# Cross terms of a split-precision product: float32r operands exchanged for bfloat16 copies

## The chip, the core and the metric

The kernel runs on one core of a Trainium2 chip. The metric is device time in microseconds (us) of one execution. Its engines are called PE (TensorE, with PEld for its weight loads), ACT (ScalarE), DVE (VectorE), POOL (GpSimd) and SP (which issues the DMAs). Each of the four compute engines runs its own instruction list strictly in the order in which the kernel wrote it (`tc.add_manual_dep` at the end of the kernel pins that order); what lets engines wait for one another are semaphores.

## The reference

Two steps follow each other on 32,768 tokens of width 192: a short causal convolution whose seven taps are softmaxed per token and head, and a feed-forward layer whose activation is h·cos(h).

```python
# x: (8, 4096, 192), weight_gen: (8, 4096, 8 heads, 7 taps)
w = softmax(weight_gen, axis=-1)
out[b, s, head] = sum_k w[b, s, head, k] * x_pad[b, s + k, head]   # 6 rows of zeros ahead of x
h = out.reshape(32768, 192) @ w_in        # w_in: 192 x 2048
g = h * cos(h)
result = g @ w_out                        # w_out: 2048 x 192
```

`w_in` and `w_out` arrive as 64-bit floats; the kernel rebuilds each value as the sum of two 32-bit parts.

## The kernel before, in words

**Work and blocks.** The 32,768 rows are cut into 64 blocks (`NB`) of 512 rows (`CT`, four rows on each of 128 partitions). The hidden width 2048 is cut into 16 chunks of 128, taken two at a time: 8 pairs (`NPAIR`) for each block. One turn of the main loop (`for i in range(N + LAG + 1)`, `N` = 512) handles one pair of one block, and each engine gets a fixed list of instructions for it. I call such a turn an iteration.

**The two products.** Each operand is split into a high part (float32r, the precision that PE keeps of a 32-bit number) and a low part, the remainder. The first product h = x·w_in is then the sum high·high (the main term) and two cross terms, low x by high w and high x by low w. Since the contraction is 192 = 128 + 64 long and PE is used as two halves of 64 rows, `ffn_in_first` issues 3 pairs of matmuls and `ffn_in_second` 6 pairs, all 512 columns wide with 64 rows each; the two of a pair run in the two halves of PE at once. Of these 9 pairs an iteration, 3 are main terms (`wa_hi` or `wb_hi` by `x_hi`), and 6 are cross terms. `wa` holds the first contraction half-blocks of w_in, `wb` the middle one. The second product (`ffn_out`, L416, for the pair that was begun 6 iterations earlier) has 16 matmuls of 384 columns in float32r (`wo` by `ghi`) and 16 of 192 columns in bfloat16 (`wo_b` by `glo`).

**What happens to h.** h lies in PSUM (three buffers of two banks, `ps_h`). ACT rounds h + 0.25 to an integer (`act_turns`, L364), DVE subtracts (`dve_fraction`, L368), ACT takes the sine (`act_cos`, L372), DVE multiplies into h (`dve_g`, L375). An iteration later ACT writes the high part of g (`act_hi`, L382) and DVE the low part (`dve_lo`, L386), which frees the h buffer for PE.

**What happens to x.** POOL computes the convolution of later blocks (`attention`, L257 products and L272 sums, 13 instructions a block) and the softmax of 16 rows at a time (once in 4 blocks, with an Exp on ACT that costs two loads of its function table). PE transposes the result, one row of a block in each two iterations, into the last columns of the accumulator `acc` (L316). Every second iteration ACT copies `acc` to SBUF (`evacuate`, L439); in half of these cases POOL then adds it to the earlier half and stores it (L456, L457). In the iteration after the copy `split` makes the parts of the transposed row: ACT writes `x_hi` (L297, after its sine), POOL writes `x_lo` (L299, 128 x 256). Only the blocks 0, 1 and 2 are transposed and split as a whole (128 x 1024, with `x_lo` on DVE).

**Order on DVE and ACT.** In an iteration DVE runs L368, L386, L375; ACT runs L364, L382, L372, and behind these in turn L439 in one iteration and L297 in the next. Two iterations make the unit that repeats. I call the iteration with L439 A and the one with L297 and the split B.

**Weights.** `two_parts` turns the 64-bit words of a piece of w_in or w_out into parts: ACT, DVE three times, ACT for the high part (L143), for w_out a bfloat16 copy as well (L145), POOL for the low part (L146). w_in comes in seven such pieces, two before the first product, one more before the loop, the others in its first iterations.

Of the kernel before, what the change touches and what calls it, by code (L numbers as in the profile page):

```python
# [11 lines left out]
F32 = mybir.dt.float32  # L12
F32R = mybir.dt.float32r
I32 = mybir.dt.int32
U16 = mybir.dt.uint16
BF16 = mybir.dt.bfloat16
# [4 lines left out]
P = 128  # L21
# [22 lines left out]
def tile_softmax_conv_then_cos_ffn(  # L44
# [8 lines left out]
    nc = tc.nc  # L53
# [5 lines left out]
    F = w_in.shape[1]  # L59
# [4 lines left out]
    CT = R * P  # L64
# [12 lines left out]
    const = ctx.enter_context(tc.tile_pool(name="const", bufs=1))  # L77
    gpool = ctx.enter_context(tc.tile_pool(name="gpool", bufs=9))
    work = ctx.enter_context(tc.tile_pool(name="work", bufs=2))
# [13 lines left out]


    wa_hi = const.tile([P, F], F32R, name="wa_hi")
    wa_lo = const.tile([P, F], F32R, name="wa_lo")

    wb_hi = const.tile([P, F // 2], F32R, name="wb_hi")
    wb_lo = const.tile([P, F // 2], F32R, name="wb_lo")
    wo = const.tile([P, NFC, 2 * D], F32R, name="wo")  # L100
    wo_b = const.tile([P, NFC, D], BF16, name="wo_b")

    def words(n, home="ghi"):

        if home == "ghi":
            raw = gpool.tile([P, 2 * CW], I32, name="raw", tag=home)
        elif home == "fin":
            raw = work.tile([P, R * D], I32, name="raw", tag=home)
        else:
            raw = work.tile([P, 2 * CT], I32, name="raw", tag=home)  # L110
        return raw[:, 0:2 * n]
# [8 lines left out]
    def two_parts(raw, hi, lo, half=None):  # L120
        shape = hi.shape[1:]
        n = math.prod(shape)

        def shaped(t, steps):
            t = t.rearrange("p (n s) -> p n s", s=steps)
            return t if len(shape) == 1 else t.rearrange("p (a b) s -> p a b s", b=shape[1])

        low, top = (shaped(raw, 2)[..., k] for k in range(2))
        size, bits = (shaped(t[:, 0:n], 1)[..., 0] for t in room.pop(0))
        nc.scalar.activation(out=size.bitcast(F32), in_=top.bitcast(F32), func=AF.Abs, scale=F64_SCALE)  # L130
        yield
        nc.vector.tensor_scalar(
            out=size, in0=size, scalar1=3, scalar2=None, op0=ALU.logical_shift_left)
        yield

        nc.vector.scalar_tensor_tensor(
            out=size, in0=top, scalar=-0x80000000, in1=size, op0=ALU.bitwise_and, op1=ALU.bitwise_or)
        yield

        nc.vector.scalar_tensor_tensor(  # L140
            out=bits, in0=low, scalar=29, in1=size, op0=ALU.logical_shift_right, op1=ALU.bitwise_or)
        yield
        nc.scalar.copy(out=hi, in_=bits.bitcast(F32))  # L143
        if half is not None:
            nc.scalar.copy(out=half, in_=bits.bitcast(F32))  # L145
        nc.gpsimd.tensor_tensor(out=lo, in0=bits.bitcast(F32), in1=hi.bitcast(F32), op=ALU.subtract)  # L146

    def w_in_a(c0, c1, home="ghi"):
        raw = words(c1 - c0, home)
        for n in range(2):  # L150
            nc.sync.dma_start(out=raw[n * D2:(n + 1) * D2],
                              in_=w_in[n * P:n * P + D2, c0:c1].bitcast(I32))
        return two_parts(raw, wa_hi[:, c0:c1], wa_lo[:, c0:c1])

    w_in_odd_even = w_in.rearrange("k (a n c) -> n k a c", n=2, c=P)

    def w_in_b(j):
        raw = words(CW)
        pairs = slice(j * CW // P, (j + 1) * CW // P)
        for n in range(2):  # L160
            nc.sync.dma_start(out=raw[n * D2:(n + 1) * D2].rearrange("k (a c) -> k a c", c=2 * P),
                              in_=w_in_odd_even[1 - n, D2:P, pairs, :].bitcast(I32))
        cols = slice(j * CW, (j + 1) * CW)
        return two_parts(raw, wb_hi[:, cols], wb_lo[:, cols])

    w_out_v = w_out.rearrange("(c p) d -> p c d", p=P)

# [111 lines left out]
    xT, transposed = {}, set()  # L279

    def traded(t):

        nc.sync.keepalive_nop([nc.sync.lower_ap(t)])
# [4 lines left out]
    def parts_of(b):  # L288
        if b not in xT:
            hi = work.tile([P, 2, CT], F32R, name="x_hi")  # L290
            lo = work.tile([P, 2, CT], F32R, name="x_lo")
            xT[b] = (hi, lo)
        return xT[b]

    def split(b, t, cs, eng):
        hi, lo = parts_of(b)
        nc.scalar.copy(out=hi[:, :, cs], in_=t)  # L297
        yield
        eng.tensor_tensor(  # L299
            out=lo[:, :, cs], in0=t, in1=hi[:, :, cs].bitcast(F32), op=ALU.subtract)  # L300

# [23 lines left out]
    def chunk(pair, n):  # L325
        return slice((2 * pair + n) * P, (2 * pair + n + 1) * P)

    def ffn_in_first(i, h=None):

        b, pair = divmod(i, NPAIR)  # L330
        x_hi, x_lo = xT[b]
        if h is None:
            h = ps_h.tile([P, 2, CT], F32, name="h")
        for m, (w, v) in enumerate(((wa_hi, x_lo), (wa_lo, x_hi), (wa_hi, x_hi))):
            for q in range(2):
                rs = slice(q * D2, (q + 1) * D2)
                nc.tensor.matmul(  # L337
                    h[:, q, :], lhsT=w[rs, chunk(pair, q)], rhs=v[rs, q, :],
                    start=(m == 0), stop=False, skip_group_check=True)
        hs[i] = h  # L340
        traded(h)

    def ffn_in_second(i):

        b, pair = divmod(i, NPAIR)
        x_hi, x_lo = xT[b]
        h = hs[i]
        prods = ((wa_hi, x_lo, 0), (wa_lo, x_hi, 0), (wb_hi, x_lo, 1), (wb_lo, x_hi, 1),
                 (wa_hi, x_hi, 0), (wb_hi, x_hi, 1))
        for m, (w, v, middle) in enumerate(prods):  # L350
            for q in range(2):
                rs = slice(q * D2, (q + 1) * D2)
                cs = slice(pair * P, (pair + 1) * P) if middle else chunk(pair, 1 - q)
                nc.tensor.matmul(  # L354
                    h[:, 1 - q, :], lhsT=w[rs, cs], rhs=v[rs, q ^ middle, :],
                    start=False, stop=(m == len(prods) - 1), skip_group_check=True)
# [71 lines left out]
    def evacuate(j):  # L428
# [9 lines left out]
        if WHOLE < bt < NB:  # L438
            nc.scalar.copy(out=part, in_=acc)  # L439
            r = group % R  # L440
            splits.append(split(bt, part[:, :, 2 * D:], slice(r * P, (r + 1) * P), nc.gpsimd))
        else:
            nc.scalar.copy(out=part[:, :, 0:2 * D], in_=acc[:, :, 0:2 * D])
# [48 lines left out]
    def all_of(*steps):  # L492
# [4 lines left out]

    late = [
        (-1, 1, w_in_a, (768, 1280)), (-1, 2, w_in_b, (1,)), (-1, 2, w_out_2, (0,)),
        (0, 3, w_in_a, (1280, 1792)), (0, 3, w_out_2, (1,)), (1, 4, w_out_2, (2, "part1")),  # L500
        (1, 4, w_out_2, (3, "part1")), (2, 5, w_in_a, (1792, 2048, "fin")),
        (2, 5, w_out_2, (4, "fin")), (4, 6, w_out_2, (5, "part1")), (4, 7, w_out_2, (6, "part1")),
        (5, 8, w_out_2, (7, "fin")),
# [16 lines left out]
    next(sm0)  # L520
    load_rows(0)
    w_b0 = w_in_b(0)
    w_a0 = w_in_a(0, 256)
    sm1 = softmax(R, 3 * R, nc.gpsimd)
# [31 lines left out]
    go_on(w_a1, 1)  # L556
    all_of(mix_v)
    first = split(0, transpose_all(0), slice(0, CT), nc.vector)
    go_on(sm2, 2)
    go_on(w_a1, 3)  # L560
# [11 lines left out]
    for i in range(N + LAG + 1):  # L572
        b, pair = divmod(i, NPAIR)
# [20 lines left out]
        def products():  # L594
            if b < NB and pair == 0:
                assert b in transposed
            if whole is not None and j >= 0:

                ffn_out(j)
                ffn_in_first(i, whole)  # L600
            elif busy and EXP + 2 <= step <= EXP + 4:

                ffn_out(j, rest=False)
                ffn_in_first(i)
                ffn_out(j, rest=True)
            else:
                if i < N:
                    ffn_in_first(i, whole)
                if j >= 0:
                    ffn_out(j)  # L610
            if i < N:
                ffn_in_second(i)
            if j in stores:
                stores.pop(j)()
            if j >= 0:
                evacuate(j)
# [16 lines left out]
        if whole is not None:  # L633
            t = work.tile([P, 2, CT], F32, name="part0", bufs=3)
            nc.scalar.copy(out=t, in_=whole)
            later.append(split(b + 1, t, slice(0, CT), nc.vector))
# [64 lines left out]
```

## Time and profile before

| | |
|---|---|
| time, median of 3 runs | 2301.77 us (2301.21 to 2303.03) |
| span of the profiled execution, first to last instruction | 2300.3 us |
| the median less that span | 1.5 us |
| from the start to the first product | 28.45 us |
| 32 iterations (4 blocks) in the steady state | 138.41 us |
| repeated pieces of 32 iterations | about 15 |
| DVE instructions in a piece of 32 iterations | 99 |

Times in a timeline are a start and a duration in us, then the engine, the line of the kernel, the operation and `output<-inputs` with their shapes; a wait stands in brackets with the instruction that ended it. In the group rows the figures behind the bar are the busy time of the group in us and the mean duration of one instruction in ns, and behind the next bar the idle time ahead of them. PE's matmuls overlap one another, so the distance between their starts tells their cost, not the duration of one.

### The profile page before, as it was taken

The numbers are of one execution on the slowest core, as the hardware profiler recorded it, in microseconds if no ns is written. First come the engines' busy times: TensorE is split into PE (matmuls) and PEld (weight loads), VectorE is DVE, ScalarE is ACT, GpSimd is POOL, SyncE is SP. The second block draws the span as 40 slices with busy tenths as digits, with TensorE's granted clock in tenths as the row PEclk, the third lists the DMA queues.
The fourth block names the chain that finished last, engine by engine and source line by source line (L and its number), as shares of the span: only waits on it lengthen the run. The fifth ranks groups of instructions, "written<-read, shape, count | busy, mean of one in ns | idle before, by whom it ended". The sixth has DMA issues, their size and how long they took to land.

```text
span 2300.3 us, 60609 instructions
## 1 busy us (share of the span) xinstructions
PE 2215.2 (96%) x26504; PEld 1993.6 (87%) x26504; DVE 1905.0 (83%) x1646; ACT 1897.5 (82%) x2131; POOL 2002.3 (87%) x1461
## 2 busy tenths in 40 slices
PE   3799999999999999999999999999999999999998
PEld 2588998889888888998989988898888889899897
DVE  7788888888888888888888888888888888888886
ACT  4588888888888888888888888888888888888885
POOL 8699989999999989989899899989989899899840
PEclk8799999999999999999999999999999999999999
DMA  6211221211211211211211212212211212212100
GB/s 154 56 43 40 50 51 33 58 41 34 58 39 44 50 40 44 50 49 34 58 33 43 58 31 52 50 32 52 50 41 42 58 26 50 57 26 52 33 9 22
DMA packets 25767, 105.55 MB, mean 46 GB/s; under 512 B 2734, under 2 KB 6566, under 8 KB 25502
## 3 DMA queue, kind: packets, MB, share of 16 engines
q1 hardware_dynamic: 25502, 101.67, 18.5%
q8 instruction: 208, 3.41, 0.6%
q14 instruction: 57, 0.47, 0.1%
HBM read 76.50 MB, written 25.17 MB: 44 GB/s over the span
## 4 chain that ended last, share of the span: by engine, by line
PE 56%; POOL 22%; ACT 11%; DVE 7%; issue 4%; DMA 0%; SPq 0%; POOLq 0%; ACTq 0%; DVEq 0%
PE acc L416 26%; PE h L354 19%; PE h L337 10%; POOL pr L257 6%; POOL xa L272 6%; DVE turn L368 3%; ACT part L439 3%; ACT turn L364 3%; POOL part L456 3%; DVE glo L386 2%; POOL x_lo L299 2%; POOL xa L257 2%; POOL fin L457 2%; ACT turn L372 2%; ACT ghi L382 1%
## 5 line engine op out<-in xcount | busy, mean ns | idle before, releaser
L368 DVE TENSOR_TENSOR turn<-h,turn 128x1024 f32<-128x1024 f32 x512 | 625.8, 1222 | 309.9 <-ACT turn L364 309.9
L416 PE MATMUL acc<-wo,ghi 64*128 64x384 f32 x8144 | 815.2, 336 | 16.6 <-ACT part L439 13.5
L416 PEld LDWEIGHTS acc<-wo,ghi 64*128 64x128 f32 x8144 | 739.2, 185 | 64.2 <-ACT part L439 26.7
L272 POOL TENSOR_TENSOR xa<-xa,pr 128x768 f32<-128x768 f32 (+1 forms) x384 | 704.0, 1833 | 0.7
L372 ACT ACTIVATE turn<-turn 128x1024 f32<-128x1024 f32 x512 | 543.7, 1062 | 181.0 <-DVE turn L368 177.7
L375 DVE SCALAR_TENSOR_TENSOR h<-h,turn 128x1024 f32<-128x1024 f32 x512 | 631.0, 1232 | 54.2 <-ACT turn L372 54.2
L364 ACT ACTIVATE turn<-h 128x1024 int32<-128x1024 f32 x512 | 525.6, 1027 | 165.0 <-PE h L354 164.2
L386 DVE TENSOR_TENSOR glo<-h,ghi 128x1024 bf16<-128x1024 f32 x512 | 622.4, 1216 | 9.9 <-ACT ghi L382 9.9
L257 POOL TENSOR_TENSOR pr<-xt,taps 128x768 f32<-128x768 f32 (+1 forms) x384 | 588.2, 1532 | 11.9
L382 ACT CAST ghi<-h 128x1024 fp32r<-128x1024 f32 x512 | 518.2, 1012 | 15.5 <-DVE h L375 15.5
L416 PE MATMUL acc<-wo_b,glo 64*128 64x192 bf16 x8144 | 435.6, 243 | 0.0
L456 POOL TENSOR_TENSOR part<-part,part 128x768 f32<-128x768 f32 x126 | 233.0, 1849 | 183.0 <-ACT part L439 156.7
L416 PEld LDWEIGHTS <-glo 64*128 64x128 bf16 x8144 | 333.8, 94 | 28.5 <-issue 13.7
L337 PE MATMUL h<-x_lo,wa_hi 64*128 64x512 f32 x1024 | 216.4, 410 | 37.0 <-DVE glo L386 28.4
L354 PE MATMUL h<-x_lo,wa_hi 64*128 64x512 f32 x1024 | 251.1, 478 | 0.6
L439 ACT COPY part<-acc 128x1024 f32<-128x1024 f32 x244 | 242.9, 996 | 0.0
L354 PE MATMUL h<-x_lo,wb_hi 64*128 64x512 f32 x1024 | 209.4, 397 | 0.0
L354 PE MATMUL h<-x_hi,wa_hi 64*128 64x512 f32 x1024 | 209.1, 396 | 0.0
L337 PE MATMUL h<-x_hi,wa_hi 64*128 64x512 f32 x1024 | 208.1, 394 | 0.0
L337 PE MATMUL h<-x_hi,wa_lo 64*128 64x512 f32 x1024 | 207.4, 392 | 0.0
L354 PE MATMUL h<-x_hi,wb_hi 64*128 64x512 f32 x1024 | 206.9, 391 | 0.0
L354 PE MATMUL h<-x_hi,wb_lo 64*128 64x512 f32 x1024 | 206.4, 391 | 0.0
(69 smaller groups left out, 2097.7 us busy)
## 6 DMA issues: line engine op xcount, KB each, us to landing
xt<-in_x_dram SPq DMA_DIRECT2D x62, 960.0 KB, 6.9
out_dram<-fin SPq DMA_DIRECT2D x63, 384.0 KB, 3.4
taps<-in_weight_gen_dram SPq DMA_DIRECT2D x15, 448.0 KB, 4.7
raw<-in_moe_w_out_dram SPq DMA_DIRECT2D x8, 384.0 KB, 4.2
raw<-in_moe_w_in_dram SPq DMA_DIRECT2D x10, 256.0 KB, 10.0
xt<-in_x_dram SPq DMA_DIRECT2D x1, 768.0 KB, 10.3
xt<-in_x_dram SPq DMA_DIRECT2D x1, 540.0 KB, 5.7
raw<-in_moe_w_in_dram SPq DMA_DIRECT2D x4, 128.0 KB, 5.6
```

Source lines behind the costliest of these rows:

```text
L257: eng.tensor_tensor(out=dst.rearrange("p r (h g) -> p r h g", h=H), in0=xt[:, k + ra:k + rb, :].rearrange("p r (h g) -> p r h g", h=H), in ...
L272: eng.tensor_tensor(out=acc if k < K else xa, in0=acc, in1=old[:, ra:rb], op=ALU.add)
L337: nc.tensor.matmul(h[:, q, :], lhsT=w[rs, chunk(pair, q)], rhs=v[rs, q, :], start=(m == 0), stop=False, skip_group_check=True)
L354: nc.tensor.matmul(h[:, 1 - q, :], lhsT=w[rs, cs], rhs=v[rs, q ^ middle, :], start=False, stop=(m == len(prods) - 1), skip_group_check=True)
L364: nc.scalar.activation(out=t.bitcast(I32), in_=hs[i], func=AF.Identity, bias=0.25, scale=1.0)
L368: nc.vector.tensor_tensor(out=t, in0=hs[i], in1=t.bitcast(I32), op=ALU.subtract)
L372: nc.scalar.activation(out=t, in_=t, func=AF.Sin, bias=SIN_BIAS, scale=SIN_SCALE)
L375: nc.vector.scalar_tensor_tensor(out=hs[i], in0=hs[i], scalar=TWO_PI, in1=turns.pop(i), op0=ALU.mult, op1=ALU.mult)
L382: nc.scalar.copy(out=hi, in_=hs[i])
L386: nc.vector.tensor_tensor(out=lo, in0=hs.pop(i), in1=hi.bitcast(F32), op=ALU.subtract)
L416: nc.tensor.matmul(to, lhsT=g[rs, n, t * P:(t + 1) * P], rhs=w[rs, fc, :], start=(lo == 0 and c == 0 and (whole or s == 0)), stop=(lo == 1 ...
L439: nc.scalar.copy(out=part, in_=acc)
```

## The change

Low parts of x and of w_in are stored as bfloat16 instead of float32r. Beside them come bfloat16 copies of the high parts: `wa_b` and `wb_b` of the weights, written by ACT in `two_parts` (its argument `half` exists already for w_out), and `x_b` of x, written by DVE from `x_hi` in `split`. The cross terms take their operands from these: `wa_b` by `x_lo` and `wa_lo` by `x_b`, and so for `wb`. The main term stays as it is. The number and the shapes of the matmuls stay as they are.

```diff
-    wa_lo = const.tile([P, F], F32R, name="wa_lo")
+    wa_lo = const.tile([P, F], BF16, name="wa_lo")
+    wa_b = const.tile([P, F], BF16, name="wa_b")
...
-    wb_lo = const.tile([P, F // 2], F32R, name="wb_lo")
+    wb_lo = const.tile([P, F // 2], BF16, name="wb_lo")
+    wb_b = const.tile([P, F // 2], BF16, name="wb_b")
...
-        return two_parts(raw, wa_hi[:, c0:c1], wa_lo[:, c0:c1])
+        return two_parts(raw, wa_hi[:, c0:c1], wa_lo[:, c0:c1], wa_b[:, c0:c1])
...
     def parts_of(b):
...
-            lo = work.tile([P, 2, CT], F32R, name="x_lo")
-            xT[b] = (hi, lo)
+            lo = work.tile([P, 2, CT], BF16, name="x_lo")
+            near = work.tile([P, 2, CT], BF16, name="x_b")
+            xT[b] = (hi, lo, near)
...
     def split(b, t, cs, eng):
-        hi, lo = parts_of(b)
+        hi, lo, near = parts_of(b)
         nc.scalar.copy(out=hi[:, :, cs], in_=t)
         yield
+        nc.vector.tensor_copy(out=near[:, :, cs], in_=hi[:, :, cs].bitcast(F32))
         eng.tensor_tensor(
             out=lo[:, :, cs], in0=t, in1=hi[:, :, cs].bitcast(F32), op=ALU.subtract)
...
-        for m, (w, v) in enumerate(((wa_hi, x_lo), (wa_lo, x_hi), (wa_hi, x_hi))):
+        for m, (w, v) in enumerate(((wa_b, x_lo), (wa_lo, x_b), (wa_hi, x_hi))):
...
-        prods = ((wa_hi, x_lo, 0), (wa_lo, x_hi, 0), (wb_hi, x_lo, 1), (wb_lo, x_hi, 1),
+        prods = ((wa_b, x_lo, 0), (wa_lo, x_b, 0), (wb_b, x_lo, 1), (wb_lo, x_b, 1),
                  (wa_hi, x_hi, 0), (wb_hi, x_hi, 1))
```

Two places in the order of the instructions matter below. On DVE, in the steady state, this is an iteration A and an iteration B before; `turn`, `h`, `glo` and `ghi` are the tiles of the steps on h told above, with the number of the buffer.

```order
L386 TENSOR_TENSOR glo_16833<-h_16703,ghi_16832 128x1024
L375 SCALAR_TENSOR_TENSOR h_16768<-h_16768,turn_16830 128x1024
L368 TENSOR_TENSOR turn_16900<-h_16841,turn_16900 128x1024
L386 TENSOR_TENSOR glo_16903<-h_16768,ghi_16902 128x1024
L375 SCALAR_TENSOR_TENSOR h_16841<-h_16841,turn_16900 128x1024
L368 TENSOR_TENSOR turn_16970<-h_16909,turn_16970 128x1024
```

And now, in the lines of the changed file (L372, L390 and L379 there are L368, L386 and L375 of the kernel before):

```order
L390 TENSOR_TENSOR glo_16987<-h_16857,ghi_16986 128x1024
L379 SCALAR_TENSOR_TENSOR h_16922<-h_16922,turn_16984 128x1024
L302 CAST x_b_16571<-x_hi_16569 128x2x128
L372 TENSOR_TENSOR turn_17055<-h_16996,turn_17055 128x1024
L390 TENSOR_TENSOR glo_17058<-h_16922,ghi_17057 128x1024
L379 SCALAR_TENSOR_TENSOR h_16996<-h_16996,turn_17055 128x1024
L372 TENSOR_TENSOR turn_17125<-h_17064,turn_17125 128x1024
```

The cast to `x_b` is put between the last step of one iteration and the first of the next, once in two iterations; nothing else on DVE moves.

On PE this is the passage from the second product to `ffn_in_second` before.

```order
L416 MATMUL acc<-wo_b,glo 128x192
L354 MATMUL h<-x_lo,wa_hi 128x512 x2
L354 MATMUL h<-x_hi,wa_lo 128x512 x2
L354 MATMUL h<-x_lo,wb_hi 128x512 x2
L354 MATMUL h<-x_hi,wb_lo 128x512 x2
```

And now:

```order
L420 LDWEIGHTS glo
L420 MATMUL acc<-wo_b,glo 128x192
L358 LDWEIGHTS wa_b
L358 MATMUL h<-x_lo,wa_b 128x512
L358 LDWEIGHTS wa_b
L358 MATMUL h<-x_lo,wa_b 128x512
L358 LDWEIGHTS wa_lo
L358 MATMUL h<-x_b,wa_lo 128x512
```

The matmuls keep their order; those of the cross terms follow the bfloat16 matmuls of the second product directly, and their weight loads are now instructions of their own in the list (the trace shows a load for every matmul in both forms).

More of the change, by code (lines that the diff above doesn't have):

```diff
@@ L163, in w_in_b @@
         cols = slice(j * CW, (j + 1) * CW)
-        return two_parts(raw, wb_hi[:, cols], wb_lo[:, cols])
+        return two_parts(raw, wb_hi[:, cols], wb_lo[:, cols], wb_b[:, cols])
     w_out_v = w_out.rearrange("(c p) d -> p c d", p=P)
@@ L330, in ffn_in_first @@
         b, pair = divmod(i, NPAIR)
-        x_hi, x_lo = xT[b]
+        x_hi, x_lo, x_b = xT[b]
         if h is None:
             h = ps_h.tile([P, 2, CT], F32, name="h")
-        for m, (w, v) in enumerate(((wa_hi, x_lo), (wa_lo, x_hi), (wa_hi, x_hi))):
+        for m, (w, v) in enumerate(((wa_b, x_lo), (wa_lo, x_b), (wa_hi, x_hi))):
             for q in range(2):
@@ L345, in ffn_in_second @@
         b, pair = divmod(i, NPAIR)
-        x_hi, x_lo = xT[b]
+        x_hi, x_lo, x_b = xT[b]
         h = hs[i]
-        prods = ((wa_hi, x_lo, 0), (wa_lo, x_hi, 0), (wb_hi, x_lo, 1), (wb_lo, x_hi, 1),
+        prods = ((wa_b, x_lo, 0), (wa_lo, x_b, 0), (wb_b, x_lo, 1), (wb_lo, x_b, 1),
                  (wa_hi, x_hi, 0), (wb_hi, x_hi, 1))
```

## The prediction

> **What bounds the kernel now.** The page's busy times come first, then one steady piece of 32 iterations in the view of windows (columns: length, then busy time and count of PE, PEld, DVE, ACT, POOL, and PE's granted clock).
>
> ```profile
> PE 2215.2 (96%) x26504; PEld 1993.6 (87%) x26504; DVE 1905.0 (83%) x1646; ACT 1897.5 (82%) x2131; POOL 2002.3 (87%) x1461
> ...
> 1174.58:1312.99 138.41, 137.04 (x1664) 126.31 (x1665) 116.11 (x99) 117.54 (x132) 126.00 (x92) 1.00 0.19 45
> ```
>
> PE fills 137.04 of 138.41 us at full clock. All others are close behind, POOL at 126.00. So PE decides today, but not by much, and what counts is the rhythm in which the engines hand h on. PE's timeline of one iteration gives PE's own cost.
>
> ```profile
> 1200.04 1.57 PE L416 MATMUL acc<-wo,ghi 64*128 64x384 f32 x16
> ...
> 1201.51 0.82 PE L416 MATMUL acc<-wo_b,glo 64*128 64x192 bf16 x16
> 1202.11 0.48 PE L354 MATMUL h<-x_lo,wa_hi 64*128 64x512 f32 x2
> 1202.43 0.39 PE L354 MATMUL h<-x_hi,wa_lo 64*128 64x512 f32 x2
> ...
> 1204.29 1.57 PE L416 MATMUL acc<-wo,ghi 64*128 64x384 f32 x16
> ...
> 1206.36 0.48 PE L354 MATMUL h<-x_lo,wa_hi 64*128 64x512 f32 x2
> ```
>
> From 1202.11 to 1206.36 is one iteration: 4.25 us, so 32 of them take 136.0 and only 2.4 of the 138.41 are lost (around the Exp). The pairs of the first product start 1204.29 − 1202.43 = 1.86 us apart over 8 pairs, 0.2325 us each; the first one after bfloat16 work takes 1202.43 − 1202.11 = 0.32.
>
> The other rhythm is that of ACT and DVE. The timeline of an iteration A and the B after it, ACT and DVE alone:
>
> ```profile
> 1264.82 1.23 DVE L368 TENSOR_TENSOR turn<-h,turn 128x1024 f32<-128x1024 f32 x1 [0.66 <-ACT turn L364]
> ...
> 1266.08 1.06 ACT L372 ACTIVATE turn<-turn 128x1024 f32<-128x1024 f32 x1 [0.39 <-DVE turn L368]
> 1267.04 0.99 ACT L439 COPY part<-acc 128x1024 f32<-128x1024 f32 x1
> ...
> 1268.01 1.03 ACT L364 ACTIVATE turn<-h 128x1024 int32<-128x1024 f32 x1
> ...
> 1269.07 1.23 DVE L368 TENSOR_TENSOR turn<-h,turn 128x1024 f32<-128x1024 f32 x1 [0.66 <-ACT turn L364]
> ...
> 1270.21 1.21 DVE L386 TENSOR_TENSOR glo<-h,ghi 128x1024 bf16<-128x1024 f32 x1
> 1270.33 1.06 ACT L372 ACTIVATE turn<-turn 128x1024 f32<-128x1024 f32 x1 [0.38 <-DVE turn L368]
> ...
> 1271.42 1.23 DVE L375 SCALAR_TENSOR_TENSOR h<-h,turn 128x1024 f32<-128x1024 f32 x1
> ...
> 1273.31 1.23 DVE L368 TENSOR_TENSOR turn<-h,turn 128x1024 f32<-128x1024 f32 x1 [0.66 <-ACT turn L364]
> ```
>
> Follow who waits for whom: DVE L368, ACT L372, ACT L439, ACT L364, DVE L368, ACT L372, DVE L375. Each starts when the one ahead is done; there is no idle time in this chain. The next DVE instruction could start 1.15 us after L375 (as L386 does, 1.14 after L368), at 1272.57. So this chain needs 1272.57 − 1264.82 = 7.75 us for two iterations, while PE needs 8.50. The difference, 0.74 us ahead of the L368 at 1273.31, is spent waiting for PE through ACT. It is the only room in the chain, and the change puts its cast exactly there.
>
> **What PE gains.** A bfloat16 pair of 192 columns costs (0.82 − 0.243)/7 = 0.082 us, with 243 ns as the duration of one:
>
> ```profile
> L416 PE MATMUL acc<-wo_b,glo 64*128 64x192 bf16 x8144 | 435.6, 243 | 0.0
> ```
>
> No row has a bfloat16 pair of 512 columns. Scaled by columns it costs 0.082 × 512/192 = 0.219; the other bound is that it gains nothing, 0.2325. I take 0.22, near the bfloat16 row: 6 pairs × 0.0125 = 0.075 us an iteration. The 0.32 of the first pair goes too, since it now follows bfloat16 work with bfloat16 work: 0.0875 saved, of which 0.056 come back (today that pair starts 1202.11 − 1202.08 = 0.03 after the last bfloat16 pair, not 0.082). The sum is 0.105 us an iteration, between 0.03 and 0.11. PE would need 4.145, two iterations 8.29. The Trainium skill ("TensorE: Matmul & The Clock Gate", "Back-to-back issue gap") gives columns/2.4 + 2.5 ns, an estimate of 0.216 for 512 columns; by it PE would gain 0.13 an iteration. Its 0.0825 for 192 columns is what the row shows.
>
> **What DVE pays.** The cast, 128 x 256 from SBUF to SBUF, is not in this trace. Its nearest rows are DVE's other one-input instructions inside SBUF, L213 in the start, of 32, 64 and 128 elements: 182, 195 and 756 ns. Here is that line's answer, and DVE and POOL around the long one, and around another DVE instruction on SBUF alone:
>
> ```profile
> L213 DVE TENSOR_SCALAR den<-den x3: 182/195/756, 5.0 to 82.3; 128x32 f32<-128x32 f32 x1, 128x64 f32<-128x64 f32 x1, 128x128 f32<-128x128 f32 x1
> ...
> 82.27 0.76 DVE L213 TENSOR_SCALAR den<-den 128x128 f32<-128x128 f32 x1
> ...
> 78.33 4.61 POOL L272 TENSOR_TENSOR xa<-xa,pr 128x768 f32<-128x768 f32 x2
> ...
> 130.45 2.08 DVE L299 TENSOR_TENSOR x_lo<-part,x_hi 128x1024 fp32r<-128x1024 f32 x1
> ...
> 129.89 1.55 POOL L257 TENSOR_TENSOR xa<-xt,taps 128x768 f32<-128x768 f32 x1
> 131.41 4.02 POOL L257 TENSOR_TENSOR pr<-xt,taps 128x768 f32<-128x768 f32 x2
> ```
>
> The slope from 32 to 64 elements is 13 ns, so 128 should take some 220 ns, not 756. But POOL was inside an L272 that ended at 78.33 + 4.61 = 82.94, and DVE ended 0.09 after that. At 130.45 it is the same: POOL's instruction ends at 131.44, DVE's 1.09 later, and POOL's next pair takes 4.02 where two take 3.1. These DVE instructions and POOL's don't run side by side; the one that comes second waits for the other to end. The steps L368, L386 and L375, which have h in PSUM, show no such waits (1.21 to 1.23 throughout). So the question is what the cast meets, and it meets POOL nearly always:
>
> ```profile
> L272 POOL TENSOR_TENSOR xa<-xa,pr 128x768 f32<-128x768 f32 x378 | 700.5, 1853 | 0.6
> ...
> L257 POOL TENSOR_TENSOR pr<-xt,taps 128x768 f32<-128x768 f32 x378 | 585.1, 1548 | 11.9
> ...
> L456 POOL TENSOR_TENSOR part<-part,part 128x768 f32<-128x768 f32 x126 | 233.0, 1849 | 183.0 <-ACT part L439 156.7 <-ACT part L443 26.2
> ...
> L299 POOL TENSOR_TENSOR x_lo<-part,x_hi 128x256 fp32r<-128x256 f32 x244 | 179.7, 739 | 30.5 <-ACT x_hi L297 30.5
> L457 POOL TENSOR_TENSOR fin<-part 128x384 f32<-128x384 f32 x126 | 127.4, 1011 | 9.9
> ...
> L257 POOL TENSOR_TENSOR xa<-xt,taps 128x768 f32<-128x768 f32 x63 | 97.2, 1543 | 1.3
> ...
> L132 DVE TENSOR_SCALAR h<-h 128x256 int32<-128x256 int32 x2 | 0.9, 427 | 0.0
> ```
>
> A piece of 32 iterations is four blocks and holds 24 of L272, 28 of L257, 8 each of L456 and L457 and 16 of L299. For a cast that comes at any time, what is left of POOL's instruction is on average the sum of count × duration²/2 over the piece: (41.2 + 33.5 + 13.7 + 4.1 + 4.4)/138.4 = 0.70 us. The pair of iterations shown above would be one of the bad ones, since there the cast would come at 1272.57:
>
> ```profile
> 1272.52 1.55 POOL L257 TENSOR_TENSOR pr<-xt,taps 128x768 f32<-128x768 f32 x1
> ```
>
> After the wait, 256 elements at the slope of L213 (13 ns for 32) take 0.10; the long L213 took 0.09 after its wait where the slope gives 0.05, so I add 0.04 and say 0.15. One cast then costs the chain 0.70 + 0.15 − 0.08 (back-to-back DVE instructions overlap by that) = 0.77 us. Bounds: 0.19 if POOL is never met (0.27 − 0.08, from 182 ns plus 7 × 13), 0.35 if it also runs as slowly as L132 on 256 elements (427 ns less 0.08), and 1.9 if it met an L272 at its start each time. The Trainium skill ("SBUF — State Buffer", "Who interferes with whom") says the same of a port pair that DVE and GpSimd lock in turn for a whole instruction, and counts casts among those that can take it; that a cast does, no row here shows.
>
> **The sum for a piece of 32 iterations**, which holds 16 casts (244 rows of L299 are 15.25 such pieces). Chain of ACT and DVE: 16 × (7.75 + 0.77) = 136.3. The Exp and its table loads lie on ACT inside the chain, and two DVE instructions of the softmax come into it:
>
> ```profile
> L205 ACT ACT_TABLE_LOAD x15 | 19.2, 1283 | 0.3
> L372 ACT ACT_TABLE_LOAD x15 | 19.2, 1283 | 0.3
> L200 DVE TENSOR_REDUCE top<-taps 128x128 f32<-128x896 f32 x15 | 16.1, 1076 | 0.0
> L205 ACT ACTIVATE taps<-taps 128x896 f32<-128x896 f32 x15 | 14.3, 954 | 0.2
> L216 DVE RECIPROCAL den<-den 128x128 f32<-128x128 f32 x15 | 14.1, 943 | 0.0
> ```
>
> 1.28 + 0.95 + 1.28 less the 0.39 that ACT idles there anyway are 3.1, and 1.08 + 0.94 − 0.16 are 1.9. Together 141.3 against 138.4 now: 2.9 longer. Today these 5 us vanish in the chain's room of 0.74 per pair; then there is none. PE needs 32 × 4.145 = 132.6 and is no longer the bound.
>
> The remaining parts are small. The bfloat16 weight copies add seven ACT instructions like L143, 0.62 us or less each; the two before the first product lie where ACT waits 5.10 us for PE's transposes.
>
> ```profile
> L143 ACT CAST wa_hi<-t 128x512 fp32r<-128x512 f32 x3 | 1.9, 623 | 1.1 <-DVE t L140 1.1
> ...
> 26.12 1.01 ACT L297 CAST x_hi<-h 128x1024 fp32r<-128x1024 f32 x1 [5.10 <-PE h L307]
> ```
>
> The cast of block 0 (1024 elements, 0.6 us by L213's slope) stands ahead of the first `x_lo` and is paid, those of blocks 1 and 2 mostly lie in idle time: +2 us for the start. POOL's `x_lo` keeps its 256 elements. POOL is held up by 16 × 0.15 = 2.4 us a piece and stays at 128 of 141. The sum from the profiled span is 2300.3 + 15.25 × 2.9 + 2 = 2346.5; the runs' median lies 1.5 above that span: 2348.
>
> **The rivals.** *PE stays the bound: the casts find POOL idle or don't wait for it.* Then a pair of iterations costs the chain 7.94 to 8.10, below PE's 8.29; PE's 0.105 comes through in 29 of 32 iterations (three around the Exp go at ACT's pace): 3.0 × 15.25 = 46, less 2 for the start: 2258, or 2290 if PE gains only 0.03. For it speaks that no cast has been seen to wait; against it, the 756 ns of L213 and POOL's load. *The waits come out shorter*, since POOL's order is fixed and the cast may fall on favourable places. The point from which it decides: (138.4 − 5.0 − 124.0)/16 = 0.59 us a cast, a mean wait of 0.52 us instead of 0.70. Below, the kernel gets faster, down to PE's 2258; at 0.52 it is unchanged, and the room for that is small, since 0.2% of the time, about what a measurement here can tell from no change, is 0.3 us a piece or 0.02 us a cast. *POOL becomes the bound:* at 128 of 141 it would need 10 us more; I leave it with the slow side.
>
> **How the numbers follow.** My forecast (mean wait 0.55 to 0.90 us, so 138.9 to 144.5 us a piece; its own range 2311 to 2397): 0.61. PE stays the bound, or nearly: 0.20. Shorter waits: 0.12 for a faster kernel, 0.06 for an unchanged one. POOL or the start, slower: 0.01. So faster 0.32, same 0.06, slower 0.62. The range takes in the larger part of the fast rival and stops a little short of the slow end: 2255 to 2395.
>
> **What would show it.** If right: casts of 0.7 to 1.0 us on average in the group rows, scattered from 0.3 to 2; DVE's idle time ahead of L368, now this, mostly gone:
>
> ```profile
> DVE turn L368 <- ACT turn L364: 309.9, 436, 5.9
> ```
>
> PE waiting for DVE L386 or ACT often; bfloat16 pairs 0.22 apart; a piece of 32 iterations of about 141.3 us. I am wrong if the casts take 0.3 to 0.4 each, and PE's iterations come at 4.15; or if the casts wait as said and PE still keeps its beat, which would mean that the chain has room that I haven't seen.

## The result, and the profile after

| | before | after |
|---|---|---|
| time, median | 2302.4 us (4 runs, 2301.21 to 2304.57) | 2321.22 us (4 runs, 2320.88 to 2322.02) |
| span of the profiled execution | 2300.3 us | 2319.2 us |
| 32 iterations in the steady state | 138.41 us | 139.6 us |

The ratio of the times is 1.0085 (95% interval 1.0071 to 1.0100): slower, as forecast, but by 19 us where 46 were forecast. The page's busy times of the changed kernel, and one of its pieces of 32 iterations in the view of windows (busy time and count of PE, PEld, DVE, ACT, POOL, then PE's granted clock):

```profile
PE 2181.0 (94%) x26504; PEld 1675.9 (72%) x26504; DVE 2070.9 (89%) x1893; ACT 1887.8 (81%) x2138; POOL 2007.7 (87%) x1461
```

```profile
1185.10:1324.67 139.57, 135.08 (x1664) 104.03 (x1665) 126.67 (x115) 116.68 (x132) 126.39 (x92) 1.00 0.19 44
```

A piece is 1.2 us longer, and 15.25 pieces of 1.2 are 18 of the 19 us. PE has less to do and waits more; DVE has 16 instructions more and 10.6 us more of busy time in the piece. The groups say where these are, with idle time ahead of a group in the last column:

```profile
L372 DVE TENSOR_TENSOR turn<-h,turn 128x1024 f32<-128x1024 f32 x512 | 624.0, 1219 | 170.9 <-ACT turn L368 168.7
...
L341 PE MATMUL h<-x_lo,wa_b 64*128 64x512 bf16 x1024 | 201.5, 388 | 77.1 <-DVE glo L390 61.3 <-POOL x_lo L303 9.6 <-DVE x_lo L303 3.0
...
L302 DVE CAST x_b<-x_hi 128x256 bf16<-128x256 f32 x244 | 193.6, 798 | 0.0
```

The cast takes 798 ns on average for 256 elements. DVE's idle time ahead of its first step (L368 before, 309.9 us; L372 now) has fallen to 170.9, and PE waits 61.3 us for DVE's L390 where before it waited 28.4 for the same step (in this view: us in all, number of waits, the longest):

```profile
PE h L337 <- DVE glo L386: 28.4, 22, 6.7
```

PE's timeline of one iteration in the changed kernel, then DVE's and POOL's of two iterations and a bit:

```profile
1254.29 1.58 PE L420 MATMUL acc<-wo,ghi 64*128 64x384 f32 x16
...
1256.42 0.38 PE L358 MATMUL h<-x_lo,wa_b 64*128 64x512 bf16 x2
1256.63 0.38 PE L358 MATMUL h<-x_b,wa_lo 64*128 64x512 bf16 x2
1256.85 0.38 PE L358 MATMUL h<-x_lo,wb_b 64*128 64x512 bf16 x2
1257.07 0.38 PE L358 MATMUL h<-x_b,wb_lo 64*128 64x512 bf16 x2
...
1258.43 0.87 PE L420 MATMUL acc<-wo,ghi 64*128 64x384 f32 x8
```

```profile
1241.64 1.13 DVE L302 CAST x_b<-x_hi 128x256 bf16<-128x256 f32 x1
1242.69 1.21 DVE L372 TENSOR_TENSOR turn<-h,turn 128x1024 f32<-128x1024 f32 x1
...
1246.85 1.23 DVE L372 TENSOR_TENSOR turn<-h,turn 128x1024 f32<-128x1024 f32 x1 [0.59 <-ACT turn L368]
...
1249.20 1.23 DVE L379 SCALAR_TENSOR_TENSOR h<-h,turn 128x1024 f32<-128x1024 f32 x1
1250.34 0.28 DVE L302 CAST x_b<-x_hi 128x256 bf16<-128x256 f32 x1
1250.76 1.23 DVE L372 TENSOR_TENSOR turn<-h,turn 128x1024 f32<-128x1024 f32 x1
```

```profile
1240.78 1.83 POOL L274 TENSOR_TENSOR xa<-xa,pr 128x768 f32<-128x768 f32 x1
1242.58 0.78 POOL L303 TENSOR_TENSOR x_lo<-part,x_hi 128x256 bf16<-128x256 f32 x1
...
1248.86 1.54 POOL L259 TENSOR_TENSOR xa<-xt,taps 128x768 f32<-128x768 f32 x1
1250.36 1.67 POOL L259 TENSOR_TENSOR pr<-xt,taps 128x768 f32<-128x768 f32 x1
```

PE, where nothing holds it, now needs 4.14 us an iteration; its bfloat16 pairs start 0.21 to 0.22 apart. The cast of 1241.64 comes while POOL is inside an L274 that ends at 1242.61, and ends 0.16 after that; DVE's next step starts right behind it, with no wait for ACT. The cast of 1250.34 comes 0.06 before POOL's L259 ends, takes 0.28, and DVE even has time left before 1250.76. Same instruction, 1.13 and 0.28 us: the difference is the rest of POOL's.

### The profile page after: what moved, and what is told of

The parts are those of the page before. It is cut to its first block, busy times and chain, and to the rows that moved or that the text cites. A ratio compares the mean times of both kernels' runs of the same rounds, so it can differ in the third digit from the quotient of the medians.

```text
span 2319.2 us, 60667 instructions
## 1 busy us (share of the span) xinstructions
PE 2181.0 (94%) x26504; PEld 1675.9 (72%) x26504; DVE 2070.9 (89%) x1893; ACT 1887.8 (81%) x2138; POOL 2007.7 (87%) x1461
## 4 chain that ended last, share of the span: by engine, by line
PE 45%; DVE 20%; POOL 16%; ACT 12%; issue 5%; DMA 0%; SPq 0%; ACTq 0%; POOLq 0%; DVEq 0%
PE acc L420 23%; PE h L358 14%; DVE turn L372 8%; PE h L341 8%; POOL pr L259 5%; ACT part L443 4%; POOL xa L274 4%; ACT turn L368 4%; DVE glo L390 4%; DVE h L379 4%; DVE x_b L302 3%; POOL x_lo L303 2%; ACT turn L376 1%; POOL part L460 1%; POOL taps L224 1%
## 5 line engine op out<-in xcount | busy, mean ns | idle before, releaser
L420 PEld LDWEIGHTS acc<-wo,ghi 64*128 64x128 f32 x8144 | 730.0, 186 | 104.3 <-ACT part L443 76.3
L372 DVE TENSOR_TENSOR turn<-h,turn 128x1024 f32<-128x1024 f32 x512 | 624.0, 1219 | 170.9 <-ACT turn L368 168.7
L274 POOL TENSOR_TENSOR xa<-xa,pr 128x768 f32<-128x768 f32 (+1 forms) x384 | 699.9, 1823 | 0.7
L379 DVE SCALAR_TENSOR_TENSOR h<-h,turn 128x1024 f32<-128x1024 f32 x512 | 631.2, 1233 | 54.0 <-ACT turn L376 54.0
L390 DVE TENSOR_TENSOR glo<-h,ghi 128x1024 bf16<-128x1024 f32 x512 | 621.4, 1214 | 1.1 <-ACT ghi L386 1.1
L368 ACT ACTIVATE turn<-h 128x1024 int32<-128x1024 f32 x512 | 525.4, 1026 | 115.1 <-PE h L358 114.8
L259 POOL TENSOR_TENSOR pr<-xt,taps 128x768 f32<-128x768 f32 (+1 forms) x384 | 592.9, 1544 | 11.9
L386 ACT CAST ghi<-h 128x1024 fp32r<-128x1024 f32 x512 | 518.9, 1013 | 13.0 <-DVE h L379 13.0
L460 POOL TENSOR_TENSOR part<-part,part 128x768 f32<-128x768 f32 x126 | 232.7, 1847 | 198.2 <-ACT part L443 172.7
L358 PE MATMUL h<-x_hi,wa_hi 64*128 64x512 f32 x1024 | 300.9, 582 | 0.0
L341 PE MATMUL h<-x_hi,wa_hi 64*128 64x512 f32 x1024 | 300.5, 582 | 0.0
L341 PE MATMUL h<-x_lo,wa_b 64*128 64x512 bf16 x1024 | 201.5, 388 | 77.1 <-DVE glo L390 61.3
L303 POOL TENSOR_TENSOR x_lo<-part,x_hi 128x256 bf16<-128x256 f32 x244 | 184.8, 760 | 30.2 <-ACT x_hi L300 30.1
L341 PEld LDWEIGHTS <-wa_b 64*128 64x128 bf16 x1024 | 51.4, 93 | 218.8 <-issue 116.6
L302 DVE CAST x_b<-x_hi 128x256 bf16<-128x256 f32 (+1 forms) x247 | 198.6, 809 | 0.0
L358 PE MATMUL h<-x_lo,wa_b 64*128 64x512 bf16 x1024 | 196.8, 379 | 0.6
```

The lines of the kernel that those rows point to most:

```text
L259: eng.tensor_tensor(out=dst.rearrange("p r (h g) -> p r h g", h=H), in0=xt[:, k + ra:k + rb, :].rearrange("p r (h g) -> p r h g", h=H), in ...
L274: eng.tensor_tensor(out=acc if k < K else xa, in0=acc, in1=old[:, ra:rb], op=ALU.add)
L341: nc.tensor.matmul(h[:, q, :], lhsT=w[rs, chunk(pair, q)], rhs=v[rs, q, :], start=(m == 0), stop=False, skip_group_check=True)
L358: nc.tensor.matmul(h[:, 1 - q, :], lhsT=w[rs, cs], rhs=v[rs, q ^ middle, :], start=False, stop=(m == len(prods) - 1), skip_group_check=True)
L368: nc.scalar.activation(out=t.bitcast(I32), in_=hs[i], func=AF.Identity, bias=0.25, scale=1.0)
L372: nc.vector.tensor_tensor(out=t, in0=hs[i], in1=t.bitcast(I32), op=ALU.subtract)
```

## The experiments

The theory after the result: the loss is the wait of DVE's cast for POOL, in the chain of ACT and DVE, and PE's gain is real but paid over. The rivals: the bfloat16 matmuls bring nothing by themselves; or DVE's work, not a wait, is what costs; or the place of the cast doesn't matter.

**e1: the copy on ACT.**

```diff
         nc.scalar.copy(out=hi[:, :, cs], in_=t)
+        nc.scalar.copy(out=near[:, :, cs], in_=t)
         yield
-        nc.vector.tensor_copy(out=near[:, :, cs], in_=hi[:, :, cs].bitcast(F32))
```

> The bfloat16 copy x_b is written by ACT right behind x_hi, from the same input, and DVE has no cast. Theory (the changed kernel is slower because DVE's cast waits for POOL inside the chain of ACT and DVE): ACT's second copy of 0.39 us fits ACT's room in iteration B, the chain needs about 8.05 us for two iterations, PE about 8.25 and is the bound again; a piece of 32 iterations takes 134.5 to 135.5 us, the kernel 2245 to 2265. Rival (the bfloat16 matmuls themselves bring nothing, for instance because the float32r pair behind them pays more): 2295 to 2305, as before.

Measured: 2263.42 us (2262.89 to 2265.64), ratio 0.9833 (0.9817 to 0.9850). The change without its cast on DVE is faster than the kernel before by 1.7%. ACT's copies of 256 elements take 398 to 403 ns each; the mean of 406 in the row takes in two copies of a whole block:

```profile
L301 ACT CAST x_b<-part 128x256 bf16<-128x256 f32 (+1 forms) x246 | 99.8, 406 | 0.0
```

**e2: the same copy on DVE at the same place, by an instruction that doesn't wait.**

```diff
-        nc.vector.tensor_copy(out=near[:, :, cs], in_=hi[:, :, cs].bitcast(F32))
+        nc.vector.tensor_reduce(
+            out=near[:, :, cs], in_=hi[:, :, cs].bitcast(F32).unsqueeze(3), axis=AX.X, op=ALU.max)
```

> The same copy on DVE at the same place in DVE's list, but made by a tensor_reduce over an axis of length 1, an operation whose row of before (L200, 1.08 us each time) shows no wait for POOL. Theory (the wait for POOL is the cost, not DVE's work): the copy takes about 0.43 us each time, although its own work is longer than the cast's shortest 0.28; the chain needs 7.66 + 0.35 = 8.0 us for two iterations, PE 8.25 is the bound: 2245 to 2270. Rival (any instruction of DVE at that place costs what it costs, by its work): no better than a cast that never waits, and with 0.43 instead of 0.28 of work worse than or equal to the changed kernel: 2310 to 2325.

Measured: 2268.43 us (2267.76 to 2269.23), ratio 0.9856 (0.9841 to 0.9871). The answer for its line gives minimum, median and maximum in ns (the maximum is the copy of a whole block), and the casts of the changed kernel stand beside it:

```profile
L302 DVE TENSOR_REDUCE x_b<-x_hi x247: 407/409/1221, 26.9 to 2207.3; 128x256 bf16<-128x256 f32 x122, 128x1024 bf16<-128x1024 f32 x2
```

```profile
L302 DVE CAST x_b<-x_hi x247: 280/695/2300, 26.7 to 2258.9; 128x256 bf16<-128x256 f32 x122, 128x1024 bf16<-128x1024 f32 x2
```

More work than the cast's shortest, 0.41 against 0.28, at the same place, beside the same POOL, and the loss is gone: e2 is 1.4% faster than the kernel before. So it is not DVE's work; it is how the cast and POOL exclude each other. This is the pair that shows it.

**e3: the cast alone,** in the kernel before (the tile `x_b` has one buffer here).

```diff
         nc.scalar.copy(out=hi[:, :, cs], in_=t)
         yield
+        near = nears[b]
+        nc.vector.tensor_copy(out=near[:, :, cs], in_=hi[:, :, cs].bitcast(F32))
```

> The kernel before with the cast of x_hi to a bfloat16 tile that nobody reads, at the place where the change puts it; all matmuls in float32r as before. Theory: casts of 0.7 to 0.9 us on average; the chain takes 16 x (7.66 + 0.72) + 5.0 = 139 us a piece and PE's 8.50 binds in the pairs with short waits, so 139.5 to 142 us a piece, 2315 to 2355. Rival (the loss comes with the bfloat16 matmuls): 2300 to 2305.

Measured: 2364.3 us (2362.0 to 2365.03), ratio 1.0271 (1.0255 to 1.0286), a little beyond the expected range. The piece is 142.27 us. The casts take 892 ns on average in it, more than in the changed kernel, since they fall on other places of POOL's list.

**e4: the bfloat16 matmuls alone.**

```diff
-            near = work.tile([P, 2, CT], BF16, name="x_b")
-            xT[b] = (hi, lo, near)
+            xT[b] = (hi, lo, lo)
...
-        nc.vector.tensor_copy(out=near[:, :, cs], in_=hi[:, :, cs].bitcast(F32))
```

> The changed kernel without the cast: the second cross term reads x_lo in the place of x_b, so that term is left out of the result and another stands there; matmuls, weights and types are those of the change. Theory: PE's gain alone, 4.12 to 4.13 us an iteration and the losses of before around the Exp: 134 to 135 us a piece, 2235 to 2260. Rival (the bfloat16 matmuls bring nothing by themselves): 2295 to 2305.

Measured: 2257.78 us (2257.56 to 2258.14), ratio 0.9810 (0.9795 to 0.9824). This is PE's gain by itself, 44 us, and the mark for a version that has to make `x_b` somewhere. The piece:

```profile
1187.00:1322.80 135.80, 133.31 (x1668) 107.48 (x1666) 116.02 (x99) 116.64 (x131) 125.63 (x93) 1.00 0.19 46
```

**e5: the copy on POOL.**

```diff
-        nc.vector.tensor_copy(out=near[:, :, cs], in_=hi[:, :, cs].bitcast(F32))
+        nc.gpsimd.tensor_copy(out=near[:, :, cs], in_=hi[:, :, cs].bitcast(F32))
```

> The changed kernel with x_b written by POOL, ahead of its x_lo. Theory: the chain of ACT and DVE is free (7.66), POOL gets 16 more instructions of 0.4 to 0.7 us a piece and stands at 133 to 137 us of work where PE needs 135.8: 2262 to 2310, POOL's waits for ACT mostly gone. Rival (POOL has no room at all): above 2310.

Measured: 2261.52 us (2261.21 to 2263.93), ratio 0.9829 (0.9814 to 0.9843). POOL carries 131 of 136.1 us and still doesn't hold PE up much; its waits for ACT's copy of `acc` shrink from 172.7 us in the changed kernel to 46.5. The piece of e5 and this wait in e5 and in the changed kernel:

```profile
1185.00:1321.10 136.10, 133.34 (x1664) 106.31 (x1664) 115.97 (x98) 116.60 (x132) 130.94 (x108) 1.00 0.19 46
```

```profile
POOL part L460 <- ACT part L443: 46.5, 47, 3.6
```

```profile
POOL part L460 <- ACT part L443: 172.7, 77, 4.0
```

e1, e2 and e5 make the right `x_b` and beat both kernels. e1 and e5 stand 4 to 6 us above e4, and their intervals don't tell them apart; e2 stands 11 above it.

**e6: the cast alone, of 4 elements instead of 256,** in the kernel before.

```diff
+        near = nears[b]
+        nc.vector.tensor_copy(out=near[:, :, cs.start:cs.start + 2], in_=hi[:, :, cs.start:cs.start + 2].bitcast(F32))
```

> The kernel before with a cast of 2 x 2 instead of 2 x 128 elements, to a tile that nobody reads, at the place where the change puts it. Theory (the cost is the wait, not the elements): casts of 0.55 to 0.85 us on average, 139.5 to 142 us a piece, 2320 to 2355, near the full cast alone (2364). Rival (the cost is DVE's work): casts of 0.2 us, within the room of 0.74 us, 2300 to 2306.

Measured: 2347.57 us (2343.11 to 2349.87), ratio 1.0199 (1.0182 to 1.0216). Sixty-four times fewer elements cost 46 us, where the whole cast alone (e3) costs 62. The 16 casts of one piece:

```profile
L303 DVE CAST x_b<-x_hi x16: 156/619/1518, 1207.6 to 1333.2; 128x4 bf16<-128x4 f32 x16
```

The shortest takes 156 ns, the longest 1518. Most of what is paid is the wait.

**e7: the cast one iteration later.** `split` yields once more, and the loop makes the cast behind the `dve_g` of the next iteration.

```diff
             dve_g(i - 1)
+        all_of(*pending)
+        pending = now
...
-        all_of(*now)
+        for c in now:
+            next(c)
```

`pending` holds the splits that were begun an iteration earlier, of which only the cast is left; `next(c)` runs a split up to its `x_lo`.

> The changed kernel with the same cast on DVE one iteration later: behind L375 of iteration A instead of B (an iteration A is the one in which ACT copies acc). Theory: the cast still waits for POOL, 0.5 to 1.1 us on average, but in A the chain runs over ACT (L439) and DVE is idle 0.59 us ahead of its next L368; the chain needs the longer of 7.66 and 6.9 + cast for two iterations, mostly below PE's 8.25: 136 to 137.5 us a piece, 2262 to 2290. Rival (a wait of DVE for POOL costs the same wherever it lies): 2310 to 2330, as the changed kernel.

Measured: 2407.87 us (2406.43 to 2410.98), ratio 1.0464 (1.0448 to 1.0480). Neither theory nor rival foresaw this: the place matters, and this one is far worse. The timeline of ACT, POOL and DVE where a cast falls:

```profile
1254.34 0.99 ACT L444 COPY part<-acc 128x1024 f32<-128x1024 f32 x1
...
1255.41 1.84 POOL L461 TENSOR_TENSOR part<-part,part 128x768 f32<-128x768 f32 x1 [4.08 <-ACT part L444]
1255.61 1.79 DVE L305 CAST x_b<-x_hi 128x256 bf16<-128x256 f32 x1
...
1257.32 1.21 DVE L373 TENSOR_TENSOR turn<-h,turn 128x1024 f32<-128x1024 f32 x1
```

POOL had been idle for 4.08 us. The end of ACT's copy of `acc` releases POOL's sum at 1255.41, and the cast, which follows the same ACT steps through DVE, comes 0.20 us behind it. Of the 16 casts in a piece, seven meet this sum at 0.19 to 0.20 us from its start and one at 0.11; these eight take 1.79 to 1.90 us, and the mean rises from 0.80 to 1.28. The room that I had seen in iteration A is there (0.59 us), but a wait of 1.6 does not fit in it. Two engines that are released by the same event don't meet at random.

The later place has a second cost, which the expectation left out as well: PE's first product that reads `x_b` now waits for the cast itself. Its group in e7, and the same one in the changed kernel, which has no such wait:

```profile
L342 PE MATMUL h<-x_b,wa_lo 64*128 64x512 bf16 x1024 | 203.5, 380 | 74.6 <-DVE x_b L305 74.6
```

```profile
L341 PE MATMUL h<-x_b,wa_lo 64*128 64x512 bf16 x1024 | 197.0, 379 | 0.0
```

In the piece these are four waits of 0.94 to 1.27 us, and they follow casts of 0.28 to 1.16 us, none of the eight long ones. The piece takes 145.55 us, 9.75 more than e4's. How this divides between the long casts and PE's wait for `x_b` was not tested; the copy of e2 at the place of e7 would tell.

**e8: a fixed length in the place of the cast.** Three copies by tensor_reduce.

```diff
-        nc.vector.tensor_copy(out=near[:, :, cs], in_=hi[:, :, cs].bitcast(F32))
+        for _ in range(3):
+            nc.vector.tensor_reduce(
+                out=near[:, :, cs], in_=hi[:, :, cs].bitcast(F32).unsqueeze(3), axis=AX.X, op=ALU.max)
```

> The changed kernel with the cast replaced by three equal tensor_reduce copies, which don't wait for POOL: a fixed length of 3 x 0.33 = 0.99 us at that place of the chain, well above PE's pace, so the length of the chain itself can be read. With 7.75 us for two iterations without the copy, as forecast: 16 x 8.74 + 5.0 = 144.8 us a piece, 2402. With 7.66 as the timelines of the changed kernel suggest: 143.4 us a piece, 2380. With the softmax's 5.0 us outside the chain: below 140, under 2330.

Measured: 2430.8 us (2430.71 to 2432.12), ratio 1.0563 (1.0547 to 1.0579), a piece of 146.55 us. All three expected times are missed. The first two took the copies as 0.99 us; the three write the same tile one after the other and take 1.32, 1.24 of it in the chain:

```profile
1223.38 1.23 DVE L374 TENSOR_TENSOR turn<-h,turn 128x1024 f32<-128x1024 f32 x1 [0.59 <-ACT turn L370]
...
1226.87 1.32 DVE L303 TENSOR_REDUCE x_b<-x_hi 128x256 bf16<-128x256 f32 x3
1228.11 1.21 DVE L374 TENSOR_TENSOR turn<-h,turn 128x1024 f32<-128x1024 f32 x1
...
1232.27 1.23 DVE L374 TENSOR_TENSOR turn<-h,turn 128x1024 f32<-128x1024 f32 x1 [0.59 <-ACT turn L370]
```

From 1223.38 to 1232.27 are 8.89 us for two iterations, less 1.24 is 7.65. Sixteen such pairs are 142.24 us, so 4.3 us of the piece are left. The chain is 7.65 us long here, not 7.75, and the Exp and the softmax do lie in it, with 4.3 us where 5.0 were forecast.

## Why the prediction was right in its way and wrong in its size

- **The cast waits for POOL: right.** e2 and e6 show it by experiment, the timeline by the ends. One cast costs 0.80 us on average, 0.72 of it in the chain, where 0.77 were forecast. That the forecast and the measured average agree so well is partly luck: the same cast takes 0.89 in e3 and 1.28 in e7, where it meets POOL at other places. An average over arrivals at any time gives the order of size; in a program with a fixed rhythm the places repeat.
- **PE's gain: right.** An iteration of PE went from 4.25 to 4.13 or 4.14 (forecast 4.145). That the rival's 2258 us and e4's 2257.8 agree to a fraction of a us is luck: a piece of e4 is 2.6 us shorter than before (138.41 and 135.80) where 3.0 were forecast, which is 40 of the 44 us; the other 4 lie outside the steady pieces, where the rival had put a loss of 2.
- **The start: right.** Counted from the first product, the first 32 iterations are 1.5 us longer than before, 178.9 against 177.3 us (+2 forecast).
- **The step that failed is the length of the chain:** "Each starts when the one ahead is done; there is no idle time in this chain", and with it 7.75 us for two iterations. That was PE's pace in one of the two iterations, taken for the chain's own length, and the change makes PE faster. The chain by itself needs 7.66. In the changed kernel, from L372 at 1242.69 to the one at 1246.85 are 4.16 us, and to 1250.34, where the next DVE step could come, 7.65. Before, the first of these two iterations took 4.25, PE's pace, because ACT's L364 at 1268.01 did wait for PE, whose last matmul for that tile ends 0.05 earlier:

```profile
1267.54 0.42 PE L354 MATMUL h<-x_hi,wb_hi 64*128 64x512 f32 x2
```

  No row shows that wait as idle time, since instructions on ACT overlap. But the rows that were quoted could have told: L372 lasts 1.06 and the next starts 0.96 after it, so ACT overlaps by 0.10; L439 lasts 0.99 and L364 starts 0.97 after it, an overlap of only 0.02. Where nothing holds it, in the changed kernel, the same step overlaps by 0.10:

```profile
1244.90 0.99 ACT L443 COPY part<-acc 128x1024 f32<-128x1024 f32 x1
1245.79 1.03 ACT L368 ACTIVATE turn<-h 128x1024 int32<-128x1024 f32 x1
```

  The 0.08 between were the wait for PE. In 75 iterations A in the middle of the run before, 65 of the starts of L364 come 0.04 or 0.05 behind PE's last matmul for the tile, and only the ten others overlap L439 by 0.10 or 0.11; in the changed kernel all 75 do. Over 16 pairs the 0.09 are 1.4 us of the 1.7 us by which the piece of 141.3 was too long. The casts' 0.05 are 0.8 more and the softmax another 0.7 (below). Together that would be 2.9, and the sum by the chain alone, 16 × (7.66 + 0.72) + 4.3 = 138.4, lies 1.2 below the measured 139.6: the chain does not set the pace in every pair.
- **The Exp and the softmax: right in kind.** In e8 they add 4.3 us to the piece's chain where 5.0 were forecast. "Today these 5 us vanish in the chain's room" is too strong: 16 pairs of 8.49 are 135.8, so before the change they already cost 2.6 of the 138.41, about what the prediction itself had found lost around the Exp.
- **Where the loss lies.** PE needs 8.27 for two iterations and the chain 7.66, so the chain has room of 0.60 us, and one would think that a cast costs what it takes beyond that. These are the durations of the 16 casts in one piece, in us, sorted:

```
after: 0.28 0.28 0.43 0.43 0.46 0.50 0.58 0.60 0.82 0.99 1.06 1.13 1.15 1.18 1.25 1.58
e3:    0.28 0.45 0.47 0.47 0.53 0.59 0.62 0.82 0.94 0.96 1.05 1.06 1.19 1.58 1.59 1.66
```

  In the changed kernel eight of them stick out above 0.60 + 0.08, by 3.7 us together, and 135.8 (e4) + 3.7 = 139.5, measured 139.6. But this agreement is luck. The same sum is 1.2 us short in e3 and 1.3 in e6, and gives e2 nothing, which lost 0.65 against e4. The room is not the same in every pair. Here are the 16 pairs of one piece, each from one L368 or L372 to the next but one, in us, as worked out from the starts in the timelines:

```
                                   before     e3        e4   changed    e2
eight pairs without softmax work    67.95   68.54     66.13   67.55   66.13
pair with DVE's RECIPROCAL           8.61    9.60      8.53    9.59    8.85
pair with DVE's TENSOR_REDUCE        8.73   10.24      8.66    9.15    8.98
pair with the Exp on ACT            11.01   12.44     10.93   12.35   11.18
pair behind the Exp                  7.57    6.96      7.58    6.96    7.32
the four others                     34.55   34.48     33.97   33.97   33.99
```

  In the three pairs with softmax work the chain has no room left, and a copy costs nearly all that it takes: e2's, 0.33 in the chain, cost 0.32, 0.32 and 0.25 there, and nothing in the eight pairs without such work. In the changed kernel these three pairs lose 3.0 us against e4, the eight others 1.4, and the pair behind the Exp gives 0.6 back: 3.8, all of the difference between 135.8 and 139.6. In e3 the three lose 3.9 against before and the eight 0.6. There, with PE at its old pace, L364 is still held by PE at 40 of 75 starts in A, and three of the four ordinary pairs whose casts stick out need 7.73 or 7.74 and the cast's part in the chain: there the 7.75 of the prediction holds.
- **The point of decision: right in kind.** With 7.66 and 4.3 in the place of 7.75 and 5.0 it lies at a cast of 0.72 us instead of 0.59, a mean wait of 0.65 instead of 0.52. That is just what a cast measured, so by that sum the kernel would be unchanged. It lost 1.2 us a piece, because an average over the piece lets short casts pay for long ones, and here they do so only in part.

## What to carry to other kernels

Before an instruction is added to an engine in a chain that hands work back and forth, find the room of the chain at that very place, pair by pair and not on average, and read it by the distances between starts, since a short wait can hide in the overlap of neighbours. Ask of a length read there whether it is the chain's own or another engine's pace, above all when the change makes that engine faster. The cast on DVE from SBUF to SBUF was not to be priced by its elements here, with POOL at work nearly all the time, but by the rest of POOL's instruction; ACT, POOL itself and DVE's tensor_reduce did the same copy in 0.39 to 0.42 us each time. And where both engines follow the same event, the wait is not an average but can be the same each time: look where it falls.

## What the runs showed of the hardware that was not expected

- A copy by tensor_reduce over an axis of length 1 (float32 to bfloat16, 256 elements) took 407 to 413 ns on DVE whatever POOL did (e2), where the casts of one piece of the changed kernel took 0.28 to 1.58 us.
- POOL's cast of 256 elements took 398 ns on average (e5), as much as ACT's (median 401, e1), against 735 ns for its subtraction of two inputs of that size (e5).
- The three copies of e8, which write the same tile, did not overlap: of 0.41 to 0.42 us each, they took 1.32 together. Whether the common tile is what keeps them apart was not tested.
